# A layer-normed linear-attention and MLP block on one core: the head planned by whole tiles in place of column halves

## The chip, the cores and the metric

The program runs on one NeuronCore of a Trainium2 chip. The core has a matrix engine (TensorE, PE in the profile, with its weight loads as PEld), VectorE (DVE), ScalarE (ACT), GpSimd (POOL) and SyncE (SP), which only starts transfers. The engines take their instructions strictly in order and wait for one another through semaphores; DMA queues hang on SP and ACT. The metric is the device time of one execution in microseconds; the kernel before has a median of 142.35 us over three runs (142.25 to 142.46).

## The reference

```
xn = layernorm(x)                         # x: 2048 tokens x 448, bf16
q, k, v = xn @ wqkv                       # 16 heads of 28
pq, pk = phi(q), phi(k)                   # phi(t) = t+1 if t>0 else exp(t), plus 1e-6
s = (pq @ (pk^T v)) / (pq . sum(pk)) @ wo
g = silu((relu(xn @ w1 + b1))^2 @ w2 + b2)     # w1: 448 x 1792
out = x + s * g
```

## The kernel before, in words

Tokens are cut into 16 tiles of 128 and 4 groups of 512. Of each tile the statistics (`ln_stats`, VectorE, `st` then `mv`), the reciprocal deviation (`ln_rstd`, two ScalarE instructions, Ln into `vep` and Exp into `rstd`), the normed tile (`ln_norm`, VectorE, `xn`) and its transpose `xT` are made. The 448 columns are four chunks of the contraction, three of 128 and one of 64; `xT` holds the last one twice, on partitions 0 to 63 and 64 to 127. For that, `xn` gets a copy of its last 64 columns (`ln_twin`). Tiles 0 to 3 are transposed on TensorE (`pe_transpose`: into PSUM, then a copy to `xT`), tiles 4 to 15 by DMA.

TensorE then makes, for each group, K tiles (`kk`: tokens x 512 columns of wqkv), Q tiles (`qq`) and H tiles (`hh`: 128 hidden columns x 512 tokens, 14 of a group), each in its own PSUM bank. `pe_four` runs four of them as a quad in 14 steps; in each step two matmuls of 64 rows run side by side, on the upper and lower half of the array. `mains` runs whole 128-row chunks of one accumulation, `rests` the last 64-row chunk of two side by side. Quads are listed in `streams`; "K2 H4 K3 H6" is the first of them in the kernel before. After the four groups come the sums over tokens, the folding of the weights, and the pairs of G (second MLP matmul) and S (attention output) tiles to the end.

ScalarE and VectorE empty the banks: Exp and two VectorE passes for K and Q (`phi`), Relu with the bias and then a square for H.

The order on each engine is written by a planner (`Program.schedule`) from estimated durations. TensorE and SP keep the order in which the program lists their work; on the other engines it picks by due time or by a set priority (`prio`), and an operation can be told to come `after` others. So the emitted order is fixed before the run.

In the head of the kernel before (from `head = {}` to `pe_four(*second)`), ten warm-up matmuls read a constant that the framework sets (`junk`). Tiles 0 and 1 are normed, transposed and copied in two column halves. TensorE's order is: transposes of tile 0 and half of tile 1, K0 chunks 0 and 1, the rest of tile 1's transposes, K0's chunk 2, K1's three chunks, the transpose of the bias `b1r`; then, between the transposes of tiles 2 and 3, the three main chunks of H0 to H3 for tokens 0 to 255 (`first`); then the K rests, the H rests, and the same four H tiles for tokens 256 to 511 (`second`, a quad of 256 columns). These need the first 512 columns of w1 (`w1a`), loaded in two parts of 192 KB and two of 32 KB. ScalarE's head is the table load, then three DMA issues (x tile 1, x tiles 2 and 3, the bias); SP's is x tile 0, the K weights in three transfers, `w1a`, x tiles 4 to 7.

Of the kernel before, what the change touches and what calls it, by code (L numbers as in the profile page):

```python
# [9 lines left out]
P = 128  # L10
# [7 lines left out]
RATE = 300e3  # L18
LEAD = 8.0
# [13 lines left out]
class Op:  # L33
    def __init__(self, eng, emit, reads, writes, dur, alts, nbytes):
# [6 lines left out]
        self.after = ()  # L41
# [13 lines left out]
class Program:  # L55
# [3 lines left out]
    ENGINES = ("pe", "sp", "act", "dve", "pool")  # L59
# [27 lines left out]
    def schedule(self):  # L87
# [25 lines left out]
        free["pool"] = free["dve"] = free["act"] = free["sp"] = 0.8  # L113
# [7 lines left out]
        def ready(op):  # L121
            r = 0.0
            if any(d.end is None for d in op.after):
                return None
# [19 lines left out]
        while n:  # L144
# [69 lines left out]
            if op.nbytes:  # L214
                free[e] = st + op.dur
                s2 = max(dma_free, st + 1.75)
                dma_free = s2 + op.nbytes / RATE
                op.end = dma_free + 0.3
# [65 lines left out]
def bass_recurrent_scan__linear_attn_block__dense_activation_squared_relu__prompt_kernel(  # L284
    nc, A_x, A_wqkv, A_wo, B_x, B_w1, B_b1, B_w2, B_b2, out
):
    with ExitStack() as es:
# [4 lines left out]

        ident = sb("ident", [P, P], bf)
# [13 lines left out]
        b1r = sb("b1r", [P, P], bf)  # L307
# [33 lines left out]
        def pool(fn, writes, reads=(), dur=0.3):  # L341
            return add("pool", fn, reads, writes, dur)
# [4 lines left out]
        pool(lambda e, _: e.memset(b1r[:, :], 0.0), ["b1r"], dur=0.2)  # L347
        junk = nc.const_aps.tensor(1.0, [P, 512], bf)
# [29 lines left out]
        masks = [pool(lambda e, _: e.memset(zmask[:, :, :], 1.0), ["zmask"])]  # L378
# [19 lines left out]
        def load_x(lo, hi, eng="sp"):  # L398
            return dma(eng, x_tok[:, lo:hi, :], x_r[:, lo:hi, :], [("x", i) for i in range(lo, hi)], (hi - lo) * P * D * 2)

        def load_k(eng, w, src, name, lo, hi, eng2=None, reads=()):

            n = (hi - lo) * 2
            main = dma(
                eng, w[:, 0:3, lo:hi], src[0:384, lo:hi].rearrange("(c p) j -> p c j", p=P), [(name, 0)], 384 * n,
                reads,
# [3 lines left out]
            return main  # L410

        def load_w1(name, lo, hi, parts=1):


            for i in range(parts):
                n = (hi - lo) // parts
                c = slice(lo + i * n, lo + (i + 1) * n)
                dma(
                    "sp", w_1[:, 0:3, c], B_w1[0:384, c].rearrange("(c p) j -> p c j", p=P), [(name, 3 * i)], 768 * n
                )  # L420
# [5 lines left out]
        wnames = lambda name: [(name, i) for i in range(4 if name == "w1a" else 3)]  # L426
        table = add("act", lambda e, _: e.preload_act_table_set("natural_log_exp_and_others"), [], ["actw"], 0.1)
        table.prio = -120
        load_x(0, 1)
# [139 lines left out]
        def mains(u, ks=K3, reads=None):  # L569


            def f(e, _):
                for k in ks:
                    last = u.mm(e, 2, k, k == 0, False)
# [643 lines left out]
```

## Time and profile before

| | |
|---|---|
| median of three runs | 142.35 us |
| profiled execution | 142.46 us |
| its span | 141.2 us |
| TensorE busy | 137.8 us (98%) |
| VectorE, ScalarE, GpSimd busy | 92.0, 78.7, 22.9 us |
| granted TensorE clock | 1.00 |
| TensorE idle, 0 to 5.26 us | 0.84 us |
| TensorE idle, 132 to 141.2 us | 2.54 us |

The span is the time between the first and the last instruction of the profiled execution; the rest of its 142.46 us lies around it. A line of the timeline gives start, length, engine, line of the program, operation, output and input, and in brackets the idle time ahead of it with what ended it. A matmul's length takes in its drain, so consecutive ones overlap: at the fast clock matmuls of 512 columns start some 0.216 us apart and each shows 0.38 us. A line of the busy time by stretches gives the stretch, its length, then for TensorE, its weight loads, VectorE, ScalarE and GpSimd the busy time and the number of instructions, then the granted clock, the DMA share and GB/s.

### The profile page before, as it was taken

To read this page: it belongs to the slowest core of one execution; us is meant where nothing else is said; L and a number is where in the kernel's file an instruction comes from. 1 tells how busy PE (TensorE), PEld (TensorE's weight loads), DVE (VectorE), ACT (ScalarE), POOL (GpSimd) and SP (SyncE) were. 2 spreads that over 40 slices of the span, in tenths; PEclk is the share of its full clock that TensorE was granted. 3 is DMA by queue.
4 is the path that set the end of the run, shared out by engine and by line. 5 is a ranking of instruction groups with operands and counts; after the bars stand their busy time and mean duration, and the time that the engine had idled before them with its cause. 6 is when DMAs were issued, how large, how long until landed. Compare 5 with 4: busy or idle time off the path is not lost.

```text
span 141.2 us, 3056 instructions
## 1 busy us (share of the span) xinstructions
PE 137.8 (98%) x1225; PEld 68.4 (48%) x1225; DVE 92.0 (65%) x224; ACT 78.7 (56%) x152; POOL 22.9 (16%) x38
## 2 busy tenths in 40 slices
PE   7999999999999999999999999999999999999992
PEld 2366444444444444444445445654555555555482
DVE  0989978898878998779959910127936062452743
ACT  3558787987888897879799571333033030300220
POOL 6000000000000000000680000000001419092670
DMA  4997266999713400000000025880000202122032
GB/s 111 310 312 235 50 170 97 366 300 210 137 23 74 84 14 0 0 9 14 0 0 0 5 76 151 200 155 14 5 0 0 68 2 89 41 66 69 33 102 67
DMA packets 20210, 12.91 MB, mean 91 GB/s; under 512 B 9380, under 2 KB 19812, under 8 KB 20196
## 3 DMA queue, kind: packets, MB, share of 16 engines
q1 hardware_dynamic: 18044, 11.22, 32.1%
q10 hardware_dynamic: 2152, 1.50, 4.4%
q8 instruction: 10, 0.16, 0.5%
q14 instruction: 4, 0.03, 0.1%
HBM read 8.78 MB, written 2.10 MB: 77 GB/s over the span
## 4 chain that ended last, share of the span: by engine, by line
PE 98%; DVE 0%; issue 0%; DVEq 0%
PE pb L928 30%; PE pb L661 30%; PE pb L614 9%; PE pb L994 8%; PE pb L695 7%; PE pb L645 6%; PE pb L1035 3%; PE pb L503 1%; PE pb L701 1%; PE pb L788 1%; PE pb L749 1%; PE pb L826 0%; DVE xn L964 0%; PE pb L819 0%; DVE xn L973 0%; PE pb L784 0%
## 5 line engine op out<-in xcount | busy, mean ns | idle before, releaser
L661 PE MATMUL pb<-xT,w 64*128 64x512 bf16 (+2 forms) x408 | 51.3, 365 | 0.0
L928 PE MATMUL pb<-w,r 64*128 64x448 bf16 (+3 forms) x378 | 44.7, 343 | 0.0
L670 ACT ACTIVATE r<-pb,b1f 128x512 bf16<-128x512 f32 x56 | 35.0, 690 | 2.8 <-PE pb L661 2.8
L661 PEld LDWEIGHTS pb<-xT,w 64*128 64x128 bf16 (+1 forms) x408 | 22.8, 94 | 22.1 <-ACT r L670 0.5
L928 PEld LDWEIGHTS pb<-w,r 64*128 64x128 bf16 (+1 forms) x378 | 22.8, 95 | 20.0 <-issue 1.2
L904 ACT ACTIVATE gbuf<-gbuf 128x448 bf16<-128x448 bf16 (+1 forms) x16 | 8.6, 564 | 36.4 <-DVE gbuf L939 34.3
L939 DVE TENSOR_TENSOR gbuf<-pb,b2b 128x448 bf16<-128x448 f32 (+1 forms) x16 | 9.3, 608 | 29.3 <-PE pb L928 29.3
L973 POOL TENSOR_TENSOR xn<-xn,x_tok 128x448 bf16<-128x448 bf16 x15 | 15.0, 1030 | 48.8 <-DVE xn L964 48.8
L614 PE MATMUL pb<-w_qkv,xT 64*128 64x512 bf16 (+1 forms) x106 | 17.9, 379 | 0.0
L645 PE MATMUL pb<-xT,w_qkv 64*128 64x512 bf16 x84 | 15.5, 376 | 0.0
L678 DVE TENSOR_TENSOR r<-r 128x512 bf16<-128x512 bf16 x39 | 13.5, 416 | 0.0
L385 POOL MEMSET kvm<- 128x2048 bf16 x1 | 1.8, 1804 | 64.4 <-DVE zb L639 64.4
L451 DVE BATCH_NORM_STATS2 st<-x_tok 128x6 f32<-128x448 bf16 x16 | 9.3, 611 | 3.4 <-DMA x_tok<-in_A_x_dram 3.4
L592 ACT ACTIVATE qk<-pb 128x512 bf16<-128x512 f32 x16 | 8.9, 594 | 4.1 <-PE pb L614 3.6
L602 DVE SCALAR_TENSOR_TENSOR qk<-pb,qk 128x512 bf16<-128x512 f32 x16 | 10.7, 686 | 0.3
L994 PE MATMUL pb<-msb,pqT 64*128 64x448 bf16 (+3 forms) x93 | 10.9, 343 | 0.0
L964 DVE TENSOR_TENSOR xn<-pb,gbuf 128x448 bf16<-128x448 f32 (+2 forms) x17 | 9.2, 590 | 2.0 <-ACT gbuf L904 1.5
L679 ACT ACTIVATE r<-r 128x512 bf16<-128x512 bf16 x17 | 9.7, 651 | 0.0
L614 PEld LDWEIGHTS pb<-w_qkv,xT 64*128 64x128 bf16 (+1 forms) x106 | 6.7, 95 | 6.2 <-DVE xT L513 0.2
L695 PE MATMUL pb<-qk,xn 128*128 128x448 bf16 x48 | 9.4, 352 | 0.0
L592 ACT ACTIVATE pqT<-pb 128x512 bf16<-128x512 f32 x12 | 6.8, 597 | 3.1 <-PE pb L661 1.6
L645 PEld LDWEIGHTS pb<-xT,w_qkv 64*128 64x128 bf16 x84 | 6.0, 94 | 5.0
(77 smaller groups left out, 98.9 us busy)
## 6 DMA issues: line engine op xcount, KB each, us to landing
out_dram<-xn SPq DMA_DIRECT2D x15, 112.0 KB, 1.7
w<-in_B_w_dram SPq DMA_DIRECT2D x1, 1568.0 KB, 9.8
x_tok<-in_A_x_dram SPq DMA_DIRECT2D x3, 448.0 KB, 3.8
xT<-rows ACTq DMA_DIRECT2D x6, 112.0 KB
w<-in_B_w_dram SPq DMA_DIRECT2D x1, 576.0 KB, 5.7
xT<-rows SPq DMA_DIRECT2D x5, 112.0 KB
w_o<-in_A_wo_dram SPq DMA_DIRECT2D x1, 392.0 KB, 11.0
w_qkv<-in_A_wqkv_dram SPq DMA_DIRECT2D x1, 384.0 KB, 4.7
```

Source lines behind the costliest of these rows:

```text
L592: add("act", lambda e, _: e.activation(out=slot, in_=src(), func=AF.Exp), [buf, "actw"], [tile], 0.6)
L602: lambda e, _: e.scalar_tensor_tensor(out=slot, in0=src(), scalar=1.0 + 1e-6, in1=slot, op0=ALU.add, op1=ALU.max),
L614: return e.matmul(ps(b)[:, 0:512], xT[half[h], c, si * P : (si + 1) * P], w_qkv[half[h], c, 384 : 2 * D], start=start, stop=stop,)
L645: return e.matmul(ps(b)[:, 0:512], w_qkv[half[h], c, m * P : (m + 1) * P], xT[half[h], c, g * 512 : (g + 1) * 512], start=start, stop=stop,)
L661: return e.matmul(ps(b)[:, c0 : c0 + n], w_1[half[h], c, fi * P : (fi + 1) * P], xT[half[h], c, t : t + n], start=start, stop=stop,)
L670: lambda e, _: e.activation(out=slot, in_=ps(b)[:, 0:512], func=AF.Relu, bias=b1f[:, fi : fi + 1]),
L678: return e.tensor_tensor(out=slot, in0=slot, in1=slot, op=ALU.mult)
L679: return e.activation(out=slot, in_=slot, func=AF.Square)
L695: last = e.matmul(ps(b)[:, 0:D], xn[:, si, c * P : (c + 1) * P], pk_of(si), start=(si == 0), stop=(si == NT - 1),)
L928: return e.matmul(ps(b)[:, 0:n], r2[half[h], fi, si * P : (si + 1) * P], w_2[half[h], fi, c], start=start, stop=stop)
L973: eng, lambda e, _: e.tensor_tensor(out=ob, in0=ob, in1=x_tok[:, si, c], op=ALU.add),
L994: return e.matmul(ps(b)[:, 0:n], q, m, start=start, stop=stop)
```

## The change

The head is written by whole tiles. Norm and `xT` copy of each of tiles 0 to 3 are one instruction each; a tile's transposes are five (three of 128 columns and the last 64 columns twice, to the two halves of PSUM's partitions), so tiles 0 to 3 need no twin copy. K0 waits for all parts of its weights. H0 to H3 of group 0 are no longer split by tokens: they are an ordinary quad of 512 columns ahead of "K2 H4 K3 H6". `pe_two` runs the mains of K0 and K1, then the transposes of tiles 2 and 3, then both rests. `w1a`'s main part is one load of 384 KB. x tile 0 goes by ScalarE's queue and tile 1 by SP's; the table load comes behind ScalarE's three DMA issues. The warm-up reads a tile that VectorE sets, and two matmuls of 128 columns are added between the transposes of tiles 0 and 1. The planner's estimates (`RATE`, transfer latencies, some durations, the lead of the DMA transposes of tiles 4 to 7) differ, and the `after` ties are gone. The orders that come of it:

```
VectorE: memset junk, st0 mv0 st1 mv1 xn0 st2 xn1 mv2 st3 mv3 xT1 xn2 xn3 xT3, st4 st5 mv4 mv5,
         K0 K1 first pass, xn4 xn5, twin, K0 K1 second pass ...
ScalarE: 3 DMA issues, table load, ln/ex of 0, of 1, xT0, ln/ex of 2, of 3, xT2, Exp K0, Exp K1,
         bias copy, ln/ex of 4 and 5, Relu H0 H2 H1 H3, one Square, Exp K2 ...
TensorE: 10 warm-up, T0, 2 warm-up, T1, K0 and K1 mains, T2, T3, K rests, bias transpose,
         quad H0 H1 H2 H3, quad K2 H4 K3 H6, and from there as before
```

The list of G and S tiles at the end is the same in both programs. The diff, cut to its core:

```diff
-RATE = 300e3
+RATE = 262e3
...
-    ENGINES = ("pe", "sp", "act", "dve", "pool")
+    ENGINES = ("pe", "act", "dve", "pool", "sp")
...
-        pool(lambda e, _: e.memset(b1r[:, :], 0.0), ["b1r"], dur=0.2)
-        junk = nc.const_aps.tensor(1.0, [P, 512], bf)
+        add("dve", lambda e, _: e.memset(junk[:, :], 0.0), [], ["junk"], 0.2).prio = -1000
...
-        def load_w1(name, lo, hi, parts=1):
-
-
-            for i in range(parts):
-                n = (hi - lo) // parts
-                c = slice(lo + i * n, lo + (i + 1) * n)
-                dma(
-                    "sp", w_1[:, 0:3, c], B_w1[0:384, c].rearrange("(c p) j -> p c j", p=P), [(name, 3 * i)], 768 * n
-                )
+
+        def load_w1(name, lo, hi):
+
+
+            dma(
+                "sp", w_1[:, 0:3, lo:hi], B_w1[0:384, lo:hi].rearrange("(c p) j -> p c j", p=P), [(name, 0)],
+                768 * (hi - lo),
+            )
...
-        table = add("act", lambda e, _: e.preload_act_table_set("natural_log_exp_and_others"), [], ["actw"], 0.1)
-        table.prio = -120
-        load_x(0, 1)
-        load_x(1, 2, "act").prio = -118
+        wnames = lambda name: [(name, i) for i in range(3)]
+        load_x(0, 1, "act")
+        load_x(1, 2)
         load_k("sp", w_qkv, A_wqkv, "wk", 384, 2 * D)
-        load_x(2, 4, "act").prio = -117
-        dma("act", b1r[0:NF, :], B_b1.rearrange("(f p) -> f p", p=P), ["b1r"], F * 2, ["b1r"]).prio = -115
-        load_w1("w1a", 0, 512, 2)
+        load_x(2, 4, "act")
+        dma("act", b1r[:, :], B_b1.rearrange("(f p) -> f p", p=P), ["b1r"], F * 2).prio = -103
+        load_w1("w1a", 0, 512)
         load_x(4, 8)
         load_w1("w1b", 512, 1024)
         load_k("sp", w_qkv, A_wqkv, "wq", 0, 384)
         load_w1("w1c", 1024, F)
+        add("act", lambda e, _: e.preload_act_table_set("natural_log_exp_and_others"), [], ["actw"], 1.3).prio = -101
...
+        def pe_transpose(si, eng, prio):
             b = Buf("T")
+
+            def f(e, _):
+                v = ps(b)[:, :].bitcast(bf)
+                for c in range(3):
+                    e.transpose(v[:, c * P : (c + 1) * P], xn[:, si, c * P : (c + 1) * P], ident[:, :])
+                e.transpose(v[0:64, 3 * P : 4 * P], xn[:, si, 384:448], ident[:, :])
+                return e.transpose(v[64:P, 3 * P : 4 * P], xn[:, si, 384:448], ident[:, :])
+
+            add("pe", f, [("xn", si), "ident"], [b], 0.35)
+
             def ev(e, _):
+                src = ps(b)[:, 0:256].bitcast(bf).rearrange("p (c k) -> p c k", c=4)
+                dst = xT[:, :, si * P : (si + 1) * P]
                 if eng == "dve":
                     return e.tensor_copy(dst, src)
                 return e.activation(out=dst, in_=src, func=AF.Copy)
 
+            add(eng, ev, [b], [("xT", si)], 0.42 if eng == "dve" else 0.6).prio = prio
...
-            op.lead = LEAD + STAGGER * (3 - si % 4) if si > 7 else 4.0 + 1.4 * (7 - si)
+            op.lead = LEAD + STAGGER * (3 - si % 4)
...
+        def pe_two(a, b, between):
+
+            for u in (a, b):
+
+                def f(e, _, u=u):
+                    for k in range(3):
+                        last = u.mm(e, 2, k, k == 0, False)
+                    return last
+
+                add("pe", f, u.reads, [u.bank], 3 * MM(u.n))
+            between()
+
+            def rest(e, _):
+                a.mm(e, 0, 3, False, True)
+                return b.mm(e, 1, 3, False, True)
+
+            add("pe", rest, [r for u in (a, b) for r in [*u.reads, u.bank]], [a.bank, b.bank], MM(a.n) + 0.1)
+            a.out()
+            b.out()
...
-        head = {}
-        for i in range(4):
-            head[f"st{i}"], head[f"mv{i}"] = ln_stats(i)
-            head[f"ln{i}"], head[f"ex{i}"] = ln_rstd(i, i + 1)
-            for j in (0, 1) if i < 2 else (None,):
-                head[f"xn{i}" + ("" if j is None else str(j))] = ln_norm(i, j)
-            twin = head[f"xd{i}"] = ln_twin(i, i + 1, "dve")
-        for op in masks:
-            op.after = [twin]
-
-        def warm(n, wide=False, after=()):
+        order = ["st0", "mv0", "st1", "mv1", "xn0", "st2", "xn1", "mv2", "st3", "mv3", "xT1", "xn2", "xn3", "xT2", "xT3"]
+        at_head = {n: -100 + i for i, n in enumerate(order)}
+        for si in range(4):
+            ln_stats(si, (at_head[f"st{si}"], at_head[f"mv{si}"]))
+            ln_rstd(si, si + 1)
+            ln_norm(si, at_head[f"xn{si}"])
+
+        def warm(n, after=(), wide=False):
             b = Buf("W")
-            w = 512 if wide else P
 
             def f(e, _):
+                last = None
                 for _i in range(n):
+                    w = 512 if wide else P
                     last = e.matmul(ps(b)[:, 0:w], junk[:, 0:P], junk[:, 0:w], start=True, stop=True)
                 return last
 
-            add("pe", f, list(after), [b], n * (0.426 if wide else 0.107))
+            add("pe", f, ["junk", *after], [b], n * (0.426 if wide else 0.107))
+            return b
 
         warm(10, wide=True)
-        k0, k1 = kk(0), kk(1)
-        first = [hh(0, fi, 0) for fi in range(4)]
-        second = [hh(0, fi, 1, first[fi].bank) for fi in range(4)]
-
-        def turn(si, part, eng):
-            head[f"xT{si}{part}"] = pe_transpose(si, part, eng)
-
-        def k_mains(u, si):
-            mains(u, (0, 1), [("xT", si, 0)] + wnames("wk")[:1])
-            mains(u, (2,), [("xT", si, 1)])
-
-        def h_mains(fi):
-            xs = [("xT", i, j) for i in (0, 1) for j in (0, 1)]
-            mains(first[fi], K3, xs + [("w1a", fi // 2 * 3)])
-
-        turn(0, 0, "act")
-        turn(0, 1, "act")
-        turn(1, 0, "act")
-        mains(k0, (0, 1), [("xT", 0, 0)] + wnames("wk")[:1])
-        turn(1, 1, "dve")
-        mains(k0, (2,), [("xT", 0, 1)])
-        k_mains(k1, 1)
+        pe_transpose(0, "act", -100)
+        warm(2)
+        pe_transpose(1, "dve", at_head["xT1"])
+
+        def third_and_fourth():
+            pe_transpose(2, "act", -100)
+            pe_transpose(3, "dve", at_head["xT3"])
+
+        pe_two(kk(0), kk(1), third_and_fourth)
         bb = Buf("B1")
-        b1v = lambda: ps(bb)[:, 0 : P // 2].bitcast(bf)
-        add("pe", lambda e, _: e.transpose(b1v(), b1r[:, :], ident[:, :]), ["b1r", "ident"], [bb], 0.1)
-        head["b1"] = add(
-            "act", lambda e, _: e.activation(out=b1f[:, :], in_=b1v()[:, 0:NF], func=AF.Copy), [bb], ["b1f"], 0.2
+        add(
+            "pe", lambda e, _: e.transpose(ps(bb)[:, 0 : NF // 2].bitcast(bf), b1r[:, :], ident[0:NF, 0:NF]),
+            ["b1r", "ident"], [bb], 0.1,
         )
-        h_mains(0)
-        h_mains(1)
-        head["xT2"] = pe_transpose(2, None, "act")
-        h_mains(2)
-        head["xT3"] = pe_transpose(3, None, "dve")
-        h_mains(3)
-        n = len(pr.ops)
-        rests(k0, k1)
-        k0.out()
-        k1.out()
-        early = pr.ops[n:]
-        rests(first[0], first[2])
-        rests(first[1], first[3])
-        for eng, names in (
-            ("dve", "st0 mv0 st1 mv1 xn00 xn01 xd0 xn10 xn11 xd1 st2 mv2 xT11 st3 mv3 xn2 xd2 xn3 xd3 xT3"),
-            ("act", "ln0 ex0 ln1 ex1 xT00 xT01 xT10 ln2 ex2 b1 ln3 ex3 xT2"),
-        ):
-            ops = [head[n] for n in names.split()]
-            for i, op in enumerate(ops):
-                op.after = ops[:i]
-                op.prio = -100 + i
-        for op in early:
-            op.after = [head["xT3" if op.eng == "dve" else "xT2"]]
-        pe_four(*second)
+        add(
+            "act", lambda e, _: e.activation(out=b1f[:, :], in_=ps(bb)[:, 0 : NF // 2].bitcast(bf), func=AF.Copy), [bb],
+            ["b1f"], 0.25,
...
-            ("K2 H4 K3 H6", "H5 Q0 Q1 H7 H8 H9 Q2 H11 H10 K0' H12 H13"),
+            ("H0 H1 H2 H3 K2 H4 K3 H6", "H5 Q0 Q1 H7 H8 H9 Q2 H11 H10 K0' H12 H13"),
...
```

## The prediction

> **What bounds the kernel now.** I read the page first (busy shares, then the chain that ended last), then the busy time by stretches, then the timeline of the first 14 us, because the instruction order of the two programs differs on TensorE only in its head.
>
> ```profile
> span 141.2 us, 3056 instructions
> PE 137.8 (98%) x1225; PEld 68.4 (48%) x1225; DVE 92.0 (65%) x224; ACT 78.7 (56%) x152; POOL 22.9 (16%) x38
> PE 98%; DVE 0%; issue 0%; DVEq 0%
> ...
> 5.26:9.95 4.69, 4.69 (x36) 2.72 (x36) 4.02 (x15) 3.09 (x11) 0.00 (x0) 1.00 1.09 300
> 9.95:11.92 1.97, 1.97 (x35) 1.67 (x36) 1.88 (x6) 1.21 (x3) 0.00 (x0) 1.00 0.95 245
> 11.92:24.00 12.08, 12.08 (x116) 5.46 (x112) 11.00 (x31) 10.19 (x22) 0.00 (x0) 1.00 0.55 130
> 24.00:71.00 47.00, 47.00 (x437) 21.05 (x434) 40.27 (x100) 39.84 (x75) 2.72 (x3) 1.00 0.43 94
> ```
>
> The chain is TensorE from start to end. Its "busy" counts the modelled drain of each matmul, so I test it by work: from 11.92 to 71.01 the queue holds 18 quads of 14 steps and 21 steps of the last hidden tiles, 273 steps. The longest piece of the chain has 62 matmuls, 31 steps, in 6.69 us, 0.2158 us a step. 273 x 0.2158 = 58.91 of the 59.09 us that pass. So TensorE has some 0.2 us of slack there: whatever delays the start of the quad "K2 H4 K3 H6" delays the end, and nothing later can give it back. What remains is to find when that quad starts.
>
> The head, from the timeline (start, length, instruction):
>
> ```profile
> 0.84 4.43 PE L1035 MATMUL pb<-const-bfloat16-1.0 128*128 128x512 bf16 x10 [0.84 <-PEq L1203]
> 3.40 0.63 DVE L451 BATCH_NORM_STATS2 st<-x_tok 128x6 f32<-128x448 bf16 x1 [3.40 <-DMA x_tok<-in_A_x_dram]
> 4.06 0.18 DVE L452 BATCH_NORM_AGGREGATE mv<-st 128x2 f32<-128x6 f32 x1
> 4.16 0.59 DVE L451 BATCH_NORM_STATS2 st<-x_tok 128x6 f32<-128x448 bf16 x1
> 4.28 0.29 ACT L461 ACTIVATE vep<-mv,eps 128x1 f32<-128x1 f32 x1 [2.20 <-DVE mv L452]
> 4.61 0.20 ACT L465 ACTIVATE rstd<-vep 128x1 f32<-128x1 f32 x1
> 4.89 0.56 DVE L474 TENSOR_SCALAR xn<-x_tok,mv,rstd 128x256 bf16<-128x256 bf16 x2
> 5.25 0.84 PEld L503 LDWEIGHTS pb<-ident,xn 128*128 128x128 bf16 x6 [0.90 <-DVE xn L474]
> 6.16 0.85 PE L614 MATMUL pb<-w_qkv,xT 128*128 128x512 bf16 x2
> 6.95 1.03 PE L614 MATMUL pb<-w_qkv,xT 128*128 128x512 bf16 x4
> 8.11 0.37 DVE L474 TENSOR_SCALAR xn<-x_tok,mv,rstd 128x448 bf16<-128x448 bf16 x1
> 8.53 0.31 PEld L503 LDWEIGHTS pb<-ident,xn 128*128 128x128 bf16 x4
> 9.02 0.60 ACT L514 ACTIVATE xT<-pb 128x512 bf16<-128x512 bf16 x1 [0.26 <-PE pb L503]
> 9.73 0.42 DVE L513 COPY xT<-pb 128x512 bf16<-128x512 bf16 x1 [0.32 <-PE pb L503]
> 10.18 1.91 PE L661 MATMUL pb<-xT,w 64*128 64x256 bf16 x32
> 11.92 1.03 PE L614 MATMUL pb<-w_qkv,xT 64*128 64x512 bf16 x8
> ```
>
> The reader should see that a ladder of VectorE, ScalarE and TensorE paces the head: statistics, rstd, norm, transposes, copy. The kernel before fills TensorE's waits in it with the three main chunks of H0 to H3 for tokens 0 to 255. So when xT of tile 3 is there (9.73 + 0.42 = 10.15) only rests and the second column halves are left, until 11.92.
>
> **The change part by part.**
>
> Handoffs, read from those rows: an aggregate is issued 0.66 after its statistics and lets VectorE go on 0.10 later; Ln starts 0.22 after the aggregate's start, Exp 0.33 after Ln, a norm 0.23 after Exp; TensorE loads 0.05 after a norm or copy ends. Two transposes at the slow clock take 0.44 from load to copy (5.25 to 5.69), four at the fast one 0.49 (8.53 to 9.02, the last held by the twin copy). I take five as 0.23 + 5 x 0.107 = 0.76 slow, 0.23 + 5 x 0.056 = 0.51 fast.
>
> *Loads and warm-up.* Tile 0 comes by ScalarE's queue in place of SP's: the same 112 KB took 2.7 us there and 2.6 on SP, so statistics start at about 3.50, not 3.40. The table load now stands behind three DMA issues on ScalarE (0.43, 0.45, 0.70 long): 2.4 + 1.28 = 3.7, before Ln at 4.38, so nothing; this cover is 0.7 us. SP issues one DMA fewer ahead of x tiles 4 to 7; that only helps VectorE later. The H weights as one 384 KB load take about 4.7 us (as the K load of that size) from 2.96, and the two small parts follow by 8.7; needed at 9.6. Warm-up waits for a VectorE memset that the trace doesn't have: 0.18 (the 128x64 copy) to 1.80 (the 128x2048 POOL memset). A quarter of that memset's width scales to 0.45, the small POOL memsets take 0.20; I take 0.3 by size, so TensorE starts at 1.1 and its ten matmuls end by 5.4, as tile 0's norm does. At 0.6 the first K would start 0.1 later and still end where xT of tile 1 arrives; at 1.80 the ladder from T0 on would come about 1.2 later.
>
> *The new ladder*, in the new VectorE order (st0 mv0 st1 mv1 xn0 st2 xn1 mv2 st3 mv3 xT1 xn2 xn3 xT3), each queue strictly in order:
> - st0 3.50, mv0 4.16, st1 4.26, mv1 4.89. Ln 4.38, Exp 4.71; xn0, whole, 4.99 to 5.37.
> - T0 load 5.42, slow clock, copy by ScalarE 6.18 to 6.78. Two warm matmuls fill to 6.2.
> - st2 5.38 to 6.00, xn1 to 6.39, mv2 6.40, st3 6.50 to 7.12, mv3 7.15, then VectorE free at 7.25.
> - T1 load 6.44, done for VectorE by 7.20; xT1 7.25 to 7.67. This copy waits behind st3 and mv3.
> - K0's mains now wait for all three parts of the K weights (SP's third issue at about 2.36, 4.4 to 4.7 us to land: 6.8 to 7.0), for xT0 and for T1 to leave the queue (6.97): 6.97 to 7.62. TensorE idles 0.1; K1's mains 7.72 to 8.37. Here the lost filler shows.
> - xn2 7.68 to 8.06 and xn3 to 8.45; T2 waits for K1: 8.37, copy by ScalarE 8.88 to 9.48. T3 8.65, copy by VectorE 9.16 to 9.58. The K rests and the bias transpose fit below that.
> - H0 to H3 as one quad of 512 columns: start 9.58 + 0.05 = 9.63, 14 x 0.2158 = 3.02, so K2 starts at 12.65.
>
> 12.65 - 11.92 = +0.73. VectorE's head is 0.57 shorter (no twins, no halves; xT3 at 9.58 in place of 10.15), but the quad is all 3.02 us behind it, where 1.74 stood behind it before (10.18 to 11.92): 1.28 - 0.55 = 0.73 again.
>
> *What follows.* H4 takes H0's bank, H6 takes H2's. Relu starts 0.22 after a quad's step 11 (11.58 to 11.80 before), three took 1.84, the last 0.69, so a second one ends 0.58 + 0.69 behind the first's start: 2.37 + 0.22 + 1.27 = 3.86 after the quad's start. H4 is due at 3.02 + 0.86 = 3.88 and needs 0.05 for the handoff: +0.03. Between nothing and +0.10; I take +0.05. ScalarE is free by then (K0 and K1 Exp to 10.6, bias copy, Ln and Exp of tiles 4 and 5 to 11.7). The evacuations of group 0 come in another order, with one Square on ScalarE among them; by the same count banks come free 0.5 us or more ahead of the next quads, so I charge 0 and bound it by 0 and 0.5. Transposes by DMA of tiles 4 and 5 start about 12.7, where they started at 15.06, with K of tile 4 due near 22: hidden. From K2 on TensorE's instruction sequence is the same, the G and S order at the end included: 0. The changed planner constants emit nothing themselves.
>
> *The clock.* K0's first matmul at 6.16 took 634 ns, those from 6.95 on 379: the slow rate ends 5.3 to 6.1 us after TensorE's first matmul, though the profile's column shows 1.00. The same delay from 1.1 puts it at 6.4 to 7.2, about at K0 (6.97). I charge 0; K0 alone at the warm-up's 0.427 a step costs 3 x 0.21 = 0.63, of which 0.53 passes on (0.1 was idle); K0 and K1 together 1.16.
>
> The Trainium skill (TensorE: Matmul & The Clock Gate, Part 1: The HAM clock gate) says that the rate is raised after a busy window of about 3.4 us whose phase is free-running. It would speak against this change: the new hole at 6.2 to 6.44 may spoil a window that was full before, and the raise would come a window later, near 10. K0 and K1 would both be slow and the sum would be +0.78 + 1.16 = +1.94; by the row's fixed delay it stays +0.78.
>
> **Sum.** +0.73 + 0.05 = +0.78. The profiled execution took 142.46 (span 141.2 and 1.3 around it), 0.11 above the median of 142.35. 142.46 + 0.78 = 143.24, or 143.13 against the median; the bounds left over lie on the dear side (bank, memset, evacuations), so I say 143.2.
>
> **Rivals.**
> 1. *Slow clock or a slip through K0 and K1.* For it: two holes in TensorE that the kernel before doesn't have, and 0.1 to 0.5 us margins. Against: the holes are 0.1 to 0.3 us, and the ten warm-up matmuls are the same. +0.53 to +1.16 on top: 143.7 to 144.3.
> 2. *Banks become the bound in group 0.* VectorE is busy 11.00 and ScalarE 10.19 of the 12.08 us to 24.00, and their new order puts norms of tiles 4 and 5 ahead of K0's and K1's last pass. Against: the relus start 0.46 before K2, where it was 0.12. 0.3 to 0.6 more: 143.5 to 143.8.
> 3. *Not slower: the shorter VectorE ladder pays for the lost overlap.* It decides where H0 starts by 11.92 - 3.02 = 8.90, so xT3 must end by 8.85. For it: VectorE's head lost 0.57 us. Against: xT3 straight behind xn3 (8.45 + 0.05 + 0.51 + 0.42 = 9.43) still gives +0.58, so 0.6 us would have to leave the ladder: tile data about 0.3 earlier (st0 at 3.2) and T3 and its copy 0.3 shorter than any row here. 142.1 to 142.6.
> 4. *No effect*: the order of G and S pairs is the same in both programs; the head differs, so this needs an exact cancellation, and is part of 3.
>
> **How the numbers follow.** Forecast (+0.3 to +1.0) 0.60; rival 1 0.18; rival 2 0.12; rival 3 0.10, of which 0.03 faster by over 0.2% and 0.07 within. 0.2% is 0.28 us, more than the spread of the three runs (142.25 to 142.46) by little. Slower 0.90. The range takes in the upper end of rival 3 (142.6) and rival 1 with the bank's and memset's small extras (144.4); the forecast's own is 142.7 to 143.4.
>
> **What would show it.** In the changed profile: statistics start near 3.5; the first K matmul near 7.0 at 379 ns; a gap on TensorE ahead of K1 that ends with VectorE's copy near 7.7; the copy of tile 3 ending near 9.6, ahead of before; the first H matmul 0.05 after it, 512 columns wide; K2 at 12.65; the same sequence 0.7 to 0.8 us late to the end. K matmuls of 0.43 a step would show rival 1; TensorE waiting for ScalarE or VectorE between 13 and 24, rival 2; H0 before 8.9, rival 3. Wrong would be a head paced by a load (K weights landing after 7.0) or a quad start set by ScalarE's copy of tile 2.

## The result and the profile after

The changed kernel takes 143.51 us (median of six runs, 143.27 to 143.80); the kernel before, 142.38 (six runs, 142.25 to 142.46). The ratio is 1.0081, with a 95% interval of 1.0065 to 1.0097: slower by 0.8%. The forecast was 143.2, slower; 143.51 lies in the stated range (142.6 to 144.4), 0.1 above the 142.7 to 143.4 that the prediction called the forecast's own. The profiled execution took 143.46 with a span of 142.2, both 1.0 more than before.

The head of the page of the kernel after (span; busy time, share and instructions of each engine), and the shares of its chain:

```profile
span 142.2 us, 3026 instructions
PE 138.2 (97%) x1215; PEld 67.7 (48%) x1215; DVE 91.4 (64%) x218; ACT 78.7 (55%) x151; POOL 23.4 (16%) x37
...
PE 97%; DVE 1%; issue 0%; DVEq 0%
```

The bound is TensorE as before, so the question is again when the quad "K2 H4 K3 H6" starts. The timeline of the kernel after, VectorE's lines and TensorE's (start, length, instruction; in brackets the idle time ahead):

```profile
0.92 0.27 DVE L345 MEMSET junk<- 128x256 uint32 x1 [0.92 <-PEq L1140]
3.64 0.63 DVE L444 BATCH_NORM_STATS2 st<-x_tok 128x6 f32<-128x448 bf16 x1 [2.45 <-DMA x_tok<-in_A_x_dram]
...
7.18 0.39 DVE L497 COPY xT<-pb 128x512 bf16<-128x512 bf16 x1
7.49 0.77 DVE L466 TENSOR_SCALAR xn<-x_tok,mv,rstd 128x448 bf16<-128x448 bf16 x2
9.30 0.42 DVE L497 COPY xT<-pb 128x512 bf16<-128x512 bf16 x1 [1.04 <-PE pb L489]
```

```profile
1.25 4.45 PE L1010 MATMUL pb<-junk 128*128 128x512 bf16 x10 [1.25 <-DVE junk L345]
5.55 0.50 PE L487 MATMUL pb<-ident,xn 128*128 128x128 bf16 x3
...
6.51 0.34 PE L487 MATMUL pb<-ident,xn 128*128 128x128 bf16 x3
...
7.00 1.47 PE L597 MATMUL pb<-w_qkv,xT 128*128 128x512 bf16 x6
8.30 0.33 PE L487 MATMUL pb<-ident,xn 128*128 128x128 bf16 x3
...
8.74 0.34 PE L487 MATMUL pb<-ident,xn 128*128 128x128 bf16 x3
...
9.19 0.39 PE L597 MATMUL pb<-w_qkv,xT 64*128 64x512 bf16 x2
9.52 0.18 PE L1028 MATMUL pb<-ident,b1r 14*128 14x14 bf16 x1
9.78 3.20 PE L640 MATMUL pb<-xT,w 64*128 64x512 bf16 x28
12.81 1.03 PE L597 MATMUL pb<-w_qkv,xT 64*128 64x512 bf16 x8
13.70 1.04 PE L640 MATMUL pb<-xT,w 64*128 64x512 bf16 x8
```

K0 starts at 7.00 in place of 6.16, H0 at 9.78, and K2 at 12.81 in place of 11.92: +0.89. H4 follows 0.89 behind K2, 0.03 more than the 0.86 that K2's step of the quad takes. In the chain of waits a later piece, the same one in both programs, starts 0.92 later. Of the kernel before:

```profile
12.09 0.86 PE pb L614 x8
...
18.99 0.86 PE pb L661 x8
```

Of the kernel after:

```profile
12.98 0.86 PE pb L597 x8
...
19.91 0.86 PE pb L640 x8
```

The first long G run in the chain stands at 71.01 before and 71.93 after, and at 137.09 and 138.01 the last pieces are still 0.92 apart. So all but some 0.1 of the 1.0 us comes from the first 14 us, and nothing is given back.

### The profile page after: what moved, and what is told of

Read it like the earlier page. It is cut to its first block, busy times and chain, and to the rows that moved or that the text cites. A ratio compares the mean times of both kernels' runs of the same rounds, so it can differ in the third digit from the quotient of the medians.

```text
span 142.2 us, 3026 instructions
## 1 busy us (share of the span) xinstructions
PE 138.2 (97%) x1215; PEld 67.7 (48%) x1215; DVE 91.4 (64%) x218; ACT 78.7 (55%) x151; POOL 23.4 (16%) x37
## 4 chain that ended last, share of the span: by engine, by line
PE 97%; DVE 1%; issue 0%; DVEq 0%
PE pb L905 30%; PE pb L640 30%; PE pb L597 8%; PE pb L971 8%; PE pb L672 6%; PE pb L628 6%; PE pb L1010 3%; PE pb L678 1%; PE pb L765 1%; PE pb L487 1%; PE pb L726 1%; PE pb L488 1%; PE pb L803 0%; DVE xT L497 0%; DVE xn L941 0%
## 5 line engine op out<-in xcount | busy, mean ns | idle before, releaser
L640 PE MATMUL pb<-xT,w 64*128 64x512 bf16 x392 | 50.8, 377 | 0.1
L640 PEld LDWEIGHTS pb<-xT,w 64*128 64x128 bf16 x392 | 21.5, 94 | 23.2 <-ACT r L649 0.6
L658 ACT ACTIVATE r<-r 128x512 bf16<-128x512 bf16 x18 | 10.4, 650 | 0.0
L616 DVE TENSOR_TENSOR zacc<-zacc,qk 128x448 f32<-128x448 f32 x13 | 8.1, 622 | 0.3
```

Of the source, the lines that this page charges most:

```text
L640: return e.matmul(ps(b)[:, 0:512], w_1[half[h], c, fi * P : (fi + 1) * P], xT[half[h], c, g * 512 : (g + 1) * 512], start=start, stop=stop,)
L658: return e.activation(out=slot, in_=slot, func=AF.Square)
```

## The experiments

"K0" and "K2" are the starts of their first matmul, "xT3" the end of the copy of tile 3, all of the profiled execution; "K0 to K2" is the time between. The ratio is against runs of the kernel before on the same chip. In e1_split, e4_plan, f1_whole, g3_warm5 and g4_head the profiled execution was the fastest of all, so that the starts shown for them are at the early end.

| kernel | median us (spread) | ratio (95%) | K0 | xT3 | K2 | K0 to K2 |
|---|---|---|---|---|---|---|
| before | 142.38 (142.25-142.46) | 1 | 6.16 | 10.15 | 11.92 | 5.76 |
| after | 143.51 (143.27-143.80) | 1.0081 (1.0065-1.0097) | 7.00 | 9.72 | 12.81 | 5.81 |
| e1_split | 143.83 (143.47-144.01) | 1.0098 (1.0074-1.0121) | 6.71 | 9.69 | 12.54 | 5.83 |
| e2_loads | 143.48 (143.25-143.63) | 1.0075 (1.0053-1.0097) | 6.96 | 9.68 | 12.78 | 5.82 |
| e3_const | 143.37 (143.31-143.46) | 1.0068 (1.0050-1.0087) | 6.93 | 9.66 | 12.75 | 5.82 |
| e4_plan | 143.41 (143.29-144.08) | 1.0086 (1.0061-1.0110) | 6.87 | 9.62 | 12.71 | 5.84 |
| f4_fill | 143.50 (143.26-143.97) | 1.0086 (1.0071-1.0100) | 6.68 | 9.41 | 12.49 | 5.81 |
| g2_fillplan | 143.61 (143.13-143.72) | 1.0070 (1.0043-1.0098) | 6.85 | 9.60 | 12.68 | 5.83 |
| f1_whole | 142.53 (142.38-142.77) | 1.0015 (1.0006-1.0023) | 6.34 | 10.07 | 11.85 | 5.51 |
| f2_quad | 143.93 (143.56-144.79) | 1.0128 (1.0101-1.0154) | 6.11 | 10.02 | 13.11 | 7.00 |
| g1_notwin | 142.90 (142.62-143.98) | 1.0045 (1.0020-1.0071) | 6.68 | 10.44 | 12.32 | 5.64 |
| g4_head | 144.48 (144.02-145.14) | 1.0147 (1.0114-1.0179) | 6.47 | 10.10 | 13.19 | 6.72 |
| f3_pass | 142.90 (142.85-142.97) | 1.0042 (1.0029-1.0055) | 6.27 | 10.02 | 12.42 | |
| g3_warm5 | 144.90 (144.37-145.37) | 1.0167 (1.0129-1.0205) | 7.11 | 10.66 | 13.76 | 6.65 |

### Does a later K2 reach the end? (f3_pass)

Two warm-up matmuls are put into the kernel before, ahead of K2.

```diff
         pe_four(*second)
+        warm(2, wide=True)
```

> The kernel before with two more matmuls of 512 columns on the constant ahead of the quad K2 H4 K3 H6: 2 x 0.2158 = 0.43 us of extra TensorE work at that place. Theory that nothing behind the head gives time back: 0.43 slower, 142.8. Rival that waits behind the head take a delay in: 0.1 or less.

K2 starts at 12.42, 0.50 later (0.43 for the two matmuls, the rest for short waits, the last of them of K2's weight load for a Relu). The last piece of the chain comes 0.51 later (137.60 against 137.09), the span grows by 0.5 (141.7), the median by 0.59 against 142.31 on that chip. A delay of this size ahead of K2 is paid in full: the reading that TensorE has no slack behind K2 holds.

### The quad alone, and whole tiles alone (f2_quad, f1_whole)

f2_quad is the kernel before with H0 to H3 as the 512-column quad behind xT of tile 3; column halves, twins, loads and the planner stay.

```diff
-        first = [hh(0, fi, 0) for fi in range(4)]
-        second = [hh(0, fi, 1, first[fi].bank) for fi in range(4)]
+        second = [hh(0, fi) for fi in range(4)]
...
-        h_mains(0)
-        h_mains(1)
         head["xT2"] = pe_transpose(2, None, "act")
-        h_mains(2)
         head["xT3"] = pe_transpose(3, None, "dve")
-        h_mains(3)
...
-        rests(first[0], first[2])
-        rests(first[1], first[3])
```

> The kernel before with the other part: H0 to H3 of group 0 as one quad of 512 columns behind xT of tile 3, nothing of them earlier; halves, twins, loads and planner stay. Theory of the lost filler, by the sum of the prediction: xT of tile 3 still ends near 10.15 (VectorE's ladder is not changed), the quad starts at 10.2 and lasts 3.02, so K2 starts near 13.2, 1.3 later, 143.6 to 143.7: slower than the changed kernel, whose ladder is 0.5 shorter. Rival that TensorE's own work is the bound from K0 on: 0.3 or less, 142.7.

f1_whole is the kernel before with tiles 0 and 1 normed, transposed and copied whole; twins and filler stay.

```diff
-            for j in (0, 1) if i < 2 else (None,):
+            for j in (None,):
...
-        turn(0, 0, "act")
-        turn(0, 1, "act")
-        turn(1, 0, "act")
-        mains(k0, (0, 1), [("xT", 0, 0)] + wnames("wk")[:1])
-        turn(1, 1, "dve")
-        mains(k0, (2,), [("xT", 0, 1)])
+        head["xT0"] = pe_transpose(0, None, "act")
+        head["xT1"] = pe_transpose(1, None, "dve")
+        k_mains(k0, 0)
         k_mains(k1, 1)
```

> The kernel before with one part of the change: tiles 0 and 1 are normed, transposed and copied whole, not in column halves; the twin copies, the split of H0 to H3, the loads and the planner stay. Theory that K0's start paces the head: xn0 5.25 instead of 5.2 for the first half, T0 held by the twin copy to 5.49, xT0 copied from about 5.85 to 6.45, K0 from 6.5 in place of 6.16, but without a hole behind it; VectorE's ladder is 0.15 shorter. K2 0.1 to 0.3 later than 11.92, 142.4 to 142.6. Rival that the halves carry most of the loss: K2 near 12.6, 143.1.

Whole tiles by themselves cost next to nothing (ratio 1.0015, K2 at 11.85): K0 starts 0.18 later, and holes that TensorE had there take it up (the bias transpose behind K1 stands at 7.83, and at 7.82 before). The quad by itself costs more than the whole change. TensorE's timeline of f2_quad shows why:

```profile
8.40 0.45 PE L503 MATMUL pb<-ident,xn 128*128 128x128 bf16 x4 [0.59 <-DVE xn L474]
9.11 0.45 PE L503 MATMUL pb<-ident,xn 128*128 128x128 bf16 x4 [0.27 <-DVE xn L474]
9.49 0.39 PE L614 MATMUL pb<-w_qkv,xT 64*128 64x512 bf16 x2
10.08 3.20 PE L661 MATMUL pb<-xT,w 64*128 64x512 bf16 x28 [0.20 <-DVE xT L513]
```

Without the filler TensorE stands still 0.59, 0.27 and 0.20 us for VectorE, and the 3.03 us of the quad all lie behind xT3. K2 is at 13.11, +1.19: the prediction's 1.28 for the lost overlap, less the 0.13 by which xT3 came earlier here, and 0.04 of handoff.

The median rose by 1.62 (143.93 against 142.31), more than the expected 143.6 to 143.7, and not all of that lies in the head. The first long G run is 1.19 late as K2 is (72.20 against 71.01), but the last piece of the chain is 1.51 late (138.60 against 137.09). Between them the chain leaves TensorE once, for transfers of the attention part that VectorE waits for:

```profile
91.34 7.60 DMA xT<-tiles
...
99.17 0.63 DVE gbuf L939
99.84 5.47 PE pb L928 x56
```

This costs 0.3 there and as much in g4_head, and nothing in the kernel after or in f3_pass, whose chains stay on TensorE between 95 and 100. Why the transfers land so late in these two stays open; it is no part of the lost overlap.

### The overlap given back to the changed kernel (e1_split, f4_fill, g2_fillplan)

If the lost overlap is what the change costs, the changed kernel should gain by the split of before. e1_split gives it back, with the filler behind the transposes of tile 3:

```diff
-        pe_two(kk(0), kk(1), third_and_fourth)
+        k0, k1 = kk(0), kk(1)
+        first = [hh(0, fi, 0) for fi in range(4)]
+        second = [hh(0, fi, 1, first[fi].bank) for fi in range(4)]
+        mains(k0)
+        mains(k1)
...
+        third_and_fourth()
+        for u in first:
+            mains(u)
+        rests(k0, k1)
+        k0.out()
+        k1.out()
+        rests(first[0], first[2])
+        rests(first[1], first[3])
+        pe_four(*second)
...
-            ("H0 H1 H2 H3 K2 H4 K3 H6", "H5 Q0 Q1 H7 H8 H9 Q2 H11 H10 K0' H12 H13"),
+            ("K2 H4 K3 H6", "H5 Q0 Q1 H7 H8 H9 Q2 H11 H10 K0' H12 H13"),
```

> The changed kernel with one thing put back: H0 to H3 of group 0 split by tokens, their main chunks for tokens 0 to 255 behind the transposes of tile 3, then the rests, then the 256-column quad. Theory of the lost filler: in the changed profile TensorE has K1 done at 8.30 and the quad of 512 columns starts at 9.78. With the filler TensorE has work without a hole from 8.30: bias transpose 0.1, two sets of transposes 0.9, 12 half mains 1.31, four rests 0.45, half quad 1.51, so K2 starts near 12.55, not 12.81: 0.25 us faster than the changed kernel, near 143.25. What is left to the kernel before (11.92) is then work that starts later (K0 at 7.00 against 6.16). If the lost filler were the whole loss, K2 would come back to 11.9 and the time to 142.4. If the loss lies in banks or in the clock, no gain: 143.5.

K2 stood at 12.54, as expected, and yet the median was no better. Two readings of its profile explain both. First, the K2 gain is not the split's: in this execution K0 started at 6.71, because T0 stood 0.11 earlier (5.44) and the fast matmul rate came before it, and K0 to K2 is 5.83, against 5.81 in the kernel after. Second, H4 lost it again (TensorE's timeline of e1_split):

```profile
12.54 1.03 PE L617 MATMUL pb<-w_qkv,xT 64*128 64x512 bf16 x8
13.74 1.04 PE L662 MATMUL pb<-xT,w 64*128 64x512 bf16 x8 [0.17 <-ACT r L671]
```

H4 and H6 take the banks of H0 and H2, whose Relus came late. In this profile they follow the Exp of K1 on ScalarE without a gap, so that Exp looked like the cause. f4_fill puts the K rests ahead of the filler, so that those Exp come early, and undoes the loads and the warm-up tile too:

```diff
         mains(k0)
         mains(k1)
+        third_and_fourth()
+        rests(k0, k1)
+        k0.out()
+        k1.out()
...
-        third_and_fourth()
         for u in first:
             mains(u)
-        rests(k0, k1)
-        k0.out()
-        k1.out()
```

> The changed kernel with H0 to H3 split as in the first of these runs, but with the K rests ahead of the filler, the warm-up on the constant and the loads' order of before. If the bank wait of the first run came from the late K rests and Exp, it goes; if a late warm-up and late tile data both held T0 (each alone moved nothing), together they let T0 start near 5.3 and K0 near 6.7. K2 12.2 to 12.4 in place of 12.81: 142.9 to 143.1, still slower than before. If the filler is of no use in this order, 143.4 as with the constant alone.

K0 was 0.32 earlier (6.68) and so was K2 (12.49), but H4 still stood at 13.69. The Exp was out of the way, so it was not the cause. The chain of f4_fill shows what is: H0's own matmuls, then two Relus.

```profile
9.38 2.96 PE pb L665 x38
...
12.37 1.27 ACT r L674 x2
...
13.69 1.04 PE pb L665 x8
```

With the split only 256 columns of each H tile are left at the end, so H0 and H2 are done closer to K2: their Relus start 0.12 ahead of K2 in e1_split and f4_fill (12.42 and 12.37), 0.44 ahead in the kernel after (12.37 against 12.81). Two Relus take 1.27, so H4 comes 1.20 behind K2 with the split, and 0.89 without it. The kernel before has its Relus as late (11.80 against K2 at 11.92), but its H4 follows K2 by 0.87, for it takes other banks. g2_fillplan is f4_fill with the planner's constants of before, by which H4 and H6 get other banks:

```diff
-RATE = 262e3
+RATE = 300e3
...
-                s2 = max(dma_free, st + 1.9)
+                s2 = max(dma_free, st + 1.75)
                 dma_free = s2 + op.nbytes / RATE
-                op.end = dma_free + 0.7
+                op.end = dma_free + 0.3
```

> The kernel after with the constant as warm-up tile, the loads of before, the token split of H0 to H3 with the K rests ahead of the filler, and the planner constants of before. By these constants H4 and H6 take the banks of K0 and K1 and not those of H0 and H2. If the wait for H0's Relu (0.7 us in the run without those constants) is what gave the gain of the split back: K2 at 12.3 to 12.5, no wait over 0.1 us at H4, the first K quad after the long H run near 71.5, and 142.9 to 143.1 us. If the split's gain is lost anyway: 143.4 to 143.5.

The bank wait is gone, as said, but K2 is late, so the time misses the expectation. The chain of waits of g2_fillplan:

```profile
1.26 4.13 DMA x_tok<-in_A_x_dram
5.42 0.63 DVE st L447
6.04 0.30 DVE xn L469
6.40 0.34 PE pb L490 x3
6.91 1.43 PE pb L620 x6
...
12.84 0.86 PE pb L620 x8
13.70 0.92 PE pb L665 x8
...
19.80 0.86 PE pb L665 x8
```

The x tiles 2 and 3 landed at 5.39 in that execution. In the order st2, xn1 the norm of tile 1 stands behind st2 on VectorE, so T1 and, behind it in TensorE's queue, K0 waited for a load that neither needs. With the bank wait gone, the piece that was 19.91 in the kernel after stands at 19.80: K2's 0.13 reach it nearly whole, where e1_split and f4_fill (19.96 and 19.90) lost all.

In these three K0 to K2 is 5.81 to 5.83, split or not. From K0 on, TensorE's queue in the changed kernel is all but full: K0 and K1 1.30 (7.00 to 8.30), tile 2's transposes 0.44, tile 3's 0.45, the K rests 0.33, the quad 3.03, and 0.26 for the bias transpose and the wait for xT3. With the bias transpose at 0.11 (as in e1_split, 8.14 to 8.25), at most 0.15 of it is waiting. Hardly a hole is left there that a filler could fill.

### What makes K0 late (e2_loads, e3_const, e4_plan)

```diff
-        load_x(0, 1, "act")
-        load_x(1, 2)
+        table = add("act", lambda e, _: e.preload_act_table_set("natural_log_exp_and_others"), [], ["actw"], 0.1)
+        table.prio = -120
+        load_x(0, 1)
+        load_x(1, 2, "act")
...
-        add("act", lambda e, _: e.preload_act_table_set("natural_log_exp_and_others"), [], ["actw"], 1.3).prio = -101
```

> The changed kernel with the transfers' order of before for the first tiles: x tile 0 by SP's queue, tile 1 by ScalarE's, table load ahead of ScalarE's DMA issues; the head's order on VectorE and ScalarE is held as in the changed kernel. Ladder theory: statistics start at 3.40 instead of 3.64 and each step of the ladder follows about 0.2 earlier, K0 near 6.8, first H matmul near 9.55, K2 near 12.6: 0.2 us faster than the changed kernel, near 143.3. Rival that the K weights pace the head: K0 stays at 7.0 and nothing is gained, 143.5. Rival that loads are most of the loss: 142.7 or less.

```diff
-        add("dve", lambda e, _: e.memset(junk[:, :], 0.0), [], ["junk"], 0.2).prio = -1000
+        junk = nc.const_aps.tensor(1.0, [P, 512], bf)
```

> The changed kernel whose warm-up reads the framework's constant, so that TensorE starts at 0.84 and not at 1.25. Ladder theory: the warm-up ends at 5.1 in place of 5.5, but tile 0's norm ends at 5.49, so nothing moves: 143.5, K2 at 12.8. Clock rival: the fast rate comes 0.4 us earlier, a K0 that in some runs is slow becomes fast: 0.1 to 0.5 faster and a narrower spread than 143.27 to 143.80.

With the loads of before, statistics start at 3.40 and not at 3.64, but the ten warm-up matmuls, begun after the memset, hold T0 to 5.49. With the constant, the warm-up ends in time, but the data of tile 0 hold T0 to 5.49. Each gains 0.04 to 0.07 at K0; both together, in f4_fill, bring T0 to 5.24 and K0 to 6.68, 0.32 earlier. Two delays that hide each other, neither to be found by undoing one. The spread of e3_const is 0.15 where after's is 0.53.

e4_plan has the planner's constants of before, with the order of the head held:

```diff
-RATE = 262e3
+RATE = 300e3
...
-            op.lead = LEAD + STAGGER * (3 - si % 4)
+            op.lead = LEAD + STAGGER * (3 - si % 4) if si > 7 else 4.0 + 1.4 * (7 - si)
```

> The changed kernel with the planner's estimates of before (rate and latency of transfers, start of the queues, lead of the DMA transposes of tiles 4 to 7); the head's order on VectorE and ScalarE is held as in the changed kernel, the evacuations behind it come in another order. Ladder theory: K2 at 12.8 and the same time, 143.5 within 0.1. Rival of the banks: TensorE waits less for ScalarE and VectorE between 13 and 24, 0.2 to 0.5 faster.

143.41: no gain beyond the spread. The bank wait of 0.03 is gone (H4 0.86 behind K2), and K0 is 0.13 earlier, because the fast matmul rate came before T0 in this execution (its three transposes took 0.34).

### Which part of the shorter ladder pays (g4_head, g1_notwin)

g1_notwin is f1_whole without the twin copies, that is with five transposes for a tile; g4_head is that with the quad of f2_quad. Loads, warm-up tile, planner, and the order of statistics, norms and copies stay as before; the masks on GpSimd, tied to the twins before, come earlier.

```diff
+                def f(e, _, i=i, c=c):
+                    v = ps(b)[:, i * 64 : (i + 1) * 64].bitcast(bf)
+                    if c < 3:
+                        return e.transpose(v, xn[:, si, c * P : (c + 1) * P], ident[:, :])
+                    e.transpose(v[0:64, :], xn[:, si, 384:448], ident[:, :])
+                    return e.transpose(v[64:P, :], xn[:, si, 384:448], ident[:, :])
...
-            twin = head[f"xd{i}"] = ln_twin(i, i + 1, "dve")
```

> The kernel before with the two parts of the change that order the head: tiles 0 and 1 normed and copied whole with five transposes and no twin copies, and H0 to H3 as 512-column quad behind xT of tile 3. Loads, warm-up tile and planner constants stay as before. The theory says that these two are the change: xT of tile 3 ends 9.5 to 9.7, H0 at 9.6 to 9.8, K2 12.6 to 12.8, and 143.2 to 143.5 us. Left to loads, memset and constants together: 0 to 0.3. With the quad alone at 143.93, the shorter ladder of VectorE is then worth 0.4 to 0.7.

> The kernel before with tiles 0 and 1 whole and without the twin copies (five transposes), the filler of H0 to H3 kept. VectorE's ladder is shorter, and xT of tile 3 comes before 10.15. If the filler hides that ladder: K2 within 0.1 us of 11.9 and 142.3 to 142.6 us, no change. If the ladder still sets K2: 11.5 to 11.8, and 142.0 to 142.2 us, faster than the kernel before.

Both missed. Without the twins the kernel before is slower by 0.45% (with them, f1_whole, by 0.15%), and in g4_head their absence doesn't bring xT3 forward at all: 10.10, against 10.02 in f2_quad with its twins. VectorE's timeline of g4_head:

```profile
7.64 0.36 DVE L474 TENSOR_SCALAR xn<-x_tok,mv,rstd 128x448 bf16<-128x448 bf16 x1
8.67 0.40 DVE L474 TENSOR_SCALAR xn<-x_tok,mv,rstd 128x448 bf16<-128x448 bf16 x1 [0.66 <-ACT rstd L465]
9.68 0.42 DVE L513 COPY xT<-pb 128x512 bf16<-128x512 bf16 x1 [0.62 <-PE pb L505]
```

and ScalarE's, same kernel:

```profile
8.03 0.18 ACT L1060 ACTIVATE b1f<-pb 128x14 f32<-128x14 bf16 x1 [0.80 <-PE pb L1058]
8.11 0.29 ACT L461 ACTIVATE vep<-mv,eps 128x1 f32<-128x1 f32 x1
8.43 0.20 ACT L465 ACTIVATE rstd<-vep 128x1 f32<-128x1 f32 x1
```

VectorE has time to spare, but tile 3's norm waits 0.66 for ScalarE, whose Ln of tile 3 stands behind the bias copy, which waits for a transpose behind K1. The kernel after has st2 and st3 ahead of the copy of tile 1 and the bias copy behind the Exp of K0 and K1; there both norms are done at 8.26 (7.49 + 0.77) and wait for nothing. By these waits its earlier xT3 (9.72 against 10.15) comes of the order on VectorE and ScalarE, not of the missing twins; no run changes that order alone. And the twin's replacement costs TensorE. Its timeline of f1_whole, four transposes of tile 2, then the filler behind them:

```profile
8.54 0.39 PE L503 MATMUL pb<-ident,xn 128*128 128x128 bf16 x4
8.76 0.49 PE L661 MATMUL pb<-xT,w 128*128 128x256 bf16 x3
```

and of g1_notwin, five, then the same filler:

```profile
8.69 0.33 PE L503 MATMUL pb<-ident,xn 128*128 128x128 bf16 x3
8.95 0.24 PE L504 MATMUL pb<-ident,xn 128*64 128x128 bf16 x1
8.96 0.24 PE L505 MATMUL pb<-ident,xn 128*64 128x128 bf16 x1
9.13 0.50 PE L661 MATMUL pb<-xT,w 128*128 128x256 bf16 x3
```

0.44 us of TensorE's time in place of 0.22 (0.28 for tile 3): 0.16 to 0.22 more for each tile, on the engine that bounds the kernel.

g4_head's profile explains 1.6 of the 2.1 us of its median: 1.27 by K2 (13.19) and 0.29 by the late transfers that f2_quad has too (its last piece stands at 138.65, 1.56 late). Its profiled execution, 144.02, was its fastest; the slower ones have no trace. TensorE stands still there for 0.78 ahead of T0 and 0.54 ahead of T3, and a late rise of the matmul rate would cost about that much, but this wasn't seen.

### What the matmul rate can cost (g3_warm5)

```diff
-        warm(10, wide=True)
+        warm(5, wide=True)
```

> The kernel after with 5 warm-up matmuls in place of 10, so that TensorE stands still from about 3.4 to T0 at 5.5. Clock rival: the fast rate comes later than at K0; three steps of K0 at 0.427 cost 0.5 to 0.6, K1 too 1.2, the filler and the transposes more, so 144.0 to 145.4 us. If the rate before K0 is no matter for the time: 143.5 us as the kernel after.

144.90 as expected; the profiled execution, 144.37, was the fastest of its four. K0 and K1 are mostly slow. Single matmuls of K0 and K1, from narrow stretches of the timeline of g3_warm5:

```profile
7.94 0.63 PE L597 MATMUL pb<-w_qkv,xT 128*128 128x512 bf16 x1
...
8.37 0.82 PE L597 MATMUL pb<-w_qkv,xT 128*128 128x512 bf16 x2
```

The matmul at 7.94 starts 0.43 ahead of the next; the one behind that starts at 8.81 (8.37 + 0.82 - 0.38) and is fast. The six take 2.13 to tile 2's transposes (7.11 to 9.24) where after's took 1.30, and K2 is 0.95 late against after. So a slow rate in K0 and K1, rival 1's mechanism, costs about what was said (1.16 for both in full); the changed kernel, with its ten warm-up matmuls, met it at T0 only.

## Why the prediction was right, and where it wasn't

**Right.** Slower, by about the right size, and with the ladder's steps where they were said. The reading that carries it, that TensorE has no slack behind K2, is shown by f3_pass and by the constant 0.92 to the end. Step by step, predicted and measured: statistics 3.50 and 3.64; memset 0.30 and 0.27; T0 5.42 and 5.55; K0 6.97 and 7.00; xT1's copy 7.25 and 7.18; T2 8.37 and 8.30; T3 8.65 and 8.74; xT3's end 9.58 and 9.72; H0 9.63 and 9.78; K2 12.65 and 12.81; the quad 3.02 and 3.03; the bank wait 0.05 and 0.03; later evacuations and DMA transposes 0, and none seen.

**The sizes that were off.** 143.2 was said and 143.51 measured, +1.13 against the six runs of before where +0.78 was summed. K2 came 0.89 late where 0.73 was summed. The missing 0.16 is in the ladder's last rungs: T3 0.09 late, its copy 0.56 behind the load where 0.51 was taken for five transposes (the two narrow ones start only 0.27 behind the first), and H0 another 0.01. The five were costed as five even steps of 0.056; the profile shows 0.27 for three and 0.17 for two. The profiled executions differ by 1.00, of which 0.92 is traced to the head.

**The step that failed: "TensorE idles 0.1; K1's mains 7.72 to 8.37. Here the lost filler shows", and with it the sum 1.28 - 0.55 as an account of causes.** TensorE has no hole at K1: K0 and K1 run from 7.00 to 8.30 in one piece. The arithmetic comes out, because H0 does start behind xT3; but a second path, TensorE's own work behind K0, is as long to within 0.15 us, and the first path runs through K0 as well: T2 and T3 stand behind K0 and K1 in TensorE's queue, and xT3 is 2.72 to 2.75 behind K0 in six of the kernels with the changed order (all but e1_split, which has the bias transpose ahead of T2, and g3_warm5 with its slow K0 and K1). Of K2's 0.89, K0's start makes 0.84, and the way from K0 to K2 0.05 (5.81 against 5.76). That the sum came near is in part luck: its ladder carried the late K0 (6.97) to xT3, while the text put the loss down to the filler. The runs set late K0 and quad against each other; K2 by start of K0 and by the way H0 to H3 run:

| | H0 to H3 split, filler | H0 to H3 as one quad |
|---|---|---|
| K0 at 6.1 to 6.5 | 11.92 (before), 11.85 (f1_whole) | 13.11 (f2_quad), 13.19 (g4_head) |
| K0 at 6.7 to 7.0 | 12.54 (e1_split), 12.49 (f4_fill), 12.68 (g2_fillplan), 12.32 (g1_notwin) | 12.81 (after), 12.78, 12.75, 12.71 (e2 to e4) |

In the kernel before, either cause alone makes it slow. In the changed kernel the split gives nothing back, and what K0 gains K2 gains: in all seven kernels with the changed order, split or not (g3_warm5 with its slow K0 and K1 aside), K2 is 5.81 to 5.84 behind K0. None of them has K0 before 6.68, so it is not shown what the quad would cost there with K0 at 6.16. K2 lies behind the later of K0 + 5.8 (TensorE's work in the order of the changed kernel; 5.6 in g1_notwin's) and xT3 + 3.1 (the quad). K0 is 0.84 later: T0 0.30 (5.55 against 5.25, the loads and the memset each hiding the other), and 0.54 from T0 to K0 (1.45 against 0.91), where half a tile was enough for before. The traces split the 0.54: from T0 to its copy 0.79 (5.55 to 6.34, five transposes) where before took 0.44 (5.25 to 5.69, two), and from the copy to K0 0.66 (one copy of 0.60 for 512 columns) where before took 0.47 (256 columns). The rate is a part of the first: in e1_split and e4_plan, with T0 fast, the five took 0.55 and 0.56. No run undid one of these alone in the changed kernel. The prediction had K0 to within 0.03 and didn't draw from it that TensorE would then be full.

**The cause of the -0.55 was named wrongly.** "No twins, no halves" doesn't shorten the way to xT3 (g4_head 10.10, f2_quad 10.02); the order of statistics and bias copy does, by the waits that the traces show.

**Rivals.** 1: its mechanism is real (g3_warm5), but the slow rate ended before K0 here; it shows in after's T0 (three transposes in 0.50, T1's in 0.34) and, it seems, in the spread of 0.53. The narrow spread of e3_const, whose warm-up starts 0.41 earlier, fits that but is no proof. 2: no bank wait over 0.03 in the changed kernel; it appeared with the split (e1_split, f4_fill), where it took K2's gain. (The "0.46 before K2" of its text is 0.43 by its own terms, 3.02 - 2.37 - 0.22; measured 0.44.) 3 and 4: no version with the quad had H0 before 9.6.

No kernel here beat the one before.

## What to carry to other kernels

When the bounding engine is full, ask first when its first useful instruction can start and how much work stands behind it; then ask which late inputs add holes. If two delays or two paths end within a few tenths of each other, undoing one of them shows next to nothing (e2_loads, e3_const), and they have to be undone together (f4_fill). Ask also what both paths start from: here it was K0. A filler is worth only the hole that is still there, and a copy saved on an idle engine is no saving if its replacement runs on the full one (0.16 to 0.22 us for each tile here).

## What the hardware showed that was not expected

**The fast matmul rate comes at very different moments.** In every profile matmuls first start 0.43 us apart and later 0.22, while the granted clock is shown as 1.00 (0.998 in e4_plan at the lowest). In g4_head it changed in the warm-up (single matmuls from narrow stretches of its timeline):

```profile
3.35 0.69 PE L1032 MATMUL pb<-const-bfloat16-1.0 128*128 128x512 bf16 x2
...
3.66 0.82 PE L1032 MATMUL pb<-const-bfloat16-1.0 128*128 128x512 bf16 x3
```

The matmul of 3.35 has its successor at 3.66, 0.31 behind it: the change lies between the two, 2.5 to 2.8 us after the first matmul at 0.84. Before changed about K0's first matmul (6.16, 634 ns; the median of the six of K0 and K1 is 379), some 5.3 us after its own; after between T0 (5.55) and T1 (6.51); g3_warm5 at about 8.8, 7.5 us after its first at 1.25. The prediction's "same delay" from the first matmul is thus no rule. The Trainium skill (TensorE: Matmul & The Clock Gate, Part 1: The HAM clock gate) says that the activity window of about 3.4 us is free-running and that the number of slow matmuls differs from run to run of one kernel. The spread of moments agrees with that; in g4_head at most 2.8 us of work was enough, less than the page's window, and the +1.94 that the prediction worked out by it did not come about.

**The rate holds for transposes too**: the same three take 0.50 in after's T0 and 0.34 in its T1, so a late rise costs even where only transposes run.

**Two 64-column transposes cost as much as two or three of 128**: from the start of the pair to the next instruction 0.17 to 0.18 us (8.56 to 8.74 in after), where four of 128 take 0.22 to 0.28 in all.
